# A votes product moved within its step, gate operations reordered on GpSimd and VectorE, and one weight split moved behind a block's rows

## The chip, the cores and the metric

The kernel runs on one core of one Trainium2 chip. The metric is the device time in microseconds of one execution; of several executions the median is given. Engines are called as in the profile: PE (TensorE, matmuls), PEld (its weight loads), DVE (VectorE), ACT (ScalarE), POOL (GpSimd), SP (SyncE, which issues the DMAs).

## The reference, cut to what matters

Attention over pooled keys is followed by a mixture of experts in which each token goes to one expert.

```python
# attention: B=4, N=12288 queries, C=128; kv 384 x 32 positions, pooled 4 x 4 to 768 keys
kv_flat = kv_pool.reshape(B, -1, C) @ w_sr          # keys and values alike
s = scale * (q @ k.transpose(0, 2, 1))
a = np.exp(s - s.max(-1, keepdims=True)); a /= a.sum(-1, keepdims=True) + 1e-09
x = a @ v                                            # rows of 128, 49152 of them
# experts: E=8, F=1024
logits = x @ w_gate                                  # 8 logits a row
expert_idx = np.argmax(logits, axis=1)
gate_w = softmax(logits)[row, expert_idx]
y = gate_w * (np.maximum(x @ w1[expert], 0) @ w2[expert])
```

## The kernel before, in words

**Blocks and slices.** The 49152 rows are 96 blocks of 512 rows, 24 for each batch; a block is four slices of 128 rows. For a slice, PE multiplies the queries by the 768 keys into a score tile `s` of two PSUM halves (columns 0 to 383 of each half; there are two such tiles, used in turn). The columns from 384 on are free, and small products of other work are put there: `beside(t, c, part, ...)` registers a part that is called while slice c of block t issues its scores, and hands it those columns as a place. Then DVE takes the row maximum `nmax` (L361), ACT the exponential `a` (L368), the cast to float16 `ah` is done by ACT in even slices (L391) and by POOL in odd ones (L389), POOL makes the remainder (L393), and a transposing DMA on SP's queue (L394) brings both to `aT`. Two steps later the values' product follows (`block_values`: `m<-aT,v_sb`), and then the logits of the block.

**Steps.** After a start of eight short steps, a step t of nominal length `LEN` = 18.7 computes the scores of block t, the values of block t-2 and the experts of block t-8 (`LAG` = 8). The experts' work of a block is eight hidden products (`hidden_sum`, `hidden_high` = hh on ACT, `hidden_low` = hl on DVE), each followed by a second product (`moe_second`, into `y`). Hidden products, values and logits share three PSUM banks named `m`. The finished block is turned by a DMA (`planes`, `yT`), joined to rows by POOL (`block_join`, L594 twice), scaled by POOL (L598) and written by a DMA of SP (`block_out`).

**Groups.** Four blocks are a group (two at a few places). All rows of a group are first tried with one expert, the one with most votes; rows that chose another are done at the end in a tail. A group's gate runs in parts, one for each call of `gate_part`. In `gate_apart`, which all groups from the third on use: POOL adds to the sums (L466); DVE takes the maxima of the logits (L468); POOL subtracts, compares and multiplies (L470 to L472); DVE takes the index (L474) and the one-hot table (L475); a reciprocal (L477); a POOL product (L479); an exponential; and a few more. `group_count` sums the table (L715, `count`), `group_votes` is the small PE product that adds the counts over the partitions, into the columns beside a slice's scores; `group_first` reads it with five small DVE operations (L724 to L729) and leaves `first_i`, which `group_load` reads on SP to issue the loads of the expert's w1 and w2 (L510, L511). `weight_scales` and `split_expert` then make the float16 halves w1h, w1l, w2h, w2l (`split_part`; the low halves by POOL, L528, in two instructions each). The first two groups use the older `gate`, in which all these operations but the exponential are on DVE (L434 to L454).

**The order** of all instructions is written out by hand. `at(time, part, ...)` puts a part into a heap by a nominal time, and `run` calls the parts in the order of those times (equal times in the order of registration). So the time fixes the place of an instruction in the queues of its engines, each of which runs in order; it is no wait and no real time. In `plan_group`, T is the start of a step, t the step in which a group's last values come; the votes fall into step t+1. The first group has `plan_first`; the second has the branch `t < LAG`, whose T is the ninth step; 22 groups take the general branch; the last one is handled in the tail loop behind the last step. Parts of the main loop that the change's times stand among, with their nominal times in the step: last cast of the step before -0.4 and its remainder +0.45; hidden sums 1.05, 2.35, 4.7, 7.95, 10.3; slices' scores 0, 3.65, 9.25, 14.85 and their maxima 1.08 later; hl 2.4, 3.7, 6.05, 9.3; `q_scale_scores` (L325) 5.95; values 6.0 and 11.6; `planes` 6.02; `q_max` 7.35; `q_turn` 8.0; rows 15.3, 16.0 and 16.85.

## Time and profile before

| | |
|---|---|
| median of 3 runs | 1863.18 us (1863.13 to 1863.6) |
| the profiled execution | 1862.85 us, its span 1861.1 us |
| granted clock of PE | 0.998 |
| busy: PE, POOL, DVE, ACT | 1820.6, 1392.6, 1438.9, 1375.9 us |

The profile is one execution. A row of the order of time has the start and the length in us, the engine, the line, the operation, out<-in, the shapes, and in brackets how long the engine had been idle and what ended that; a row of the waits has who waited for whom, the total in us, the times and the longest. Gaps under 0.15 us are not counted as waits. The ends of matmuls are modelled and overlap the next ones.

### The profile page before, as it was taken

To read this page: it belongs to the slowest core of one execution; us is meant where nothing else is said; L and a number is where in the kernel's file an instruction comes from. 1 tells how busy PE (TensorE), PEld (TensorE's weight loads), DVE (VectorE), ACT (ScalarE), POOL (GpSimd) and SP (SyncE) were. 2 spreads that over 40 slices of the span, in tenths; PEclk is the share of its full clock that TensorE was granted. 3 is DMA by queue.
4 is the path that set the end of the run, shared out by engine and by line. 5 is a ranking of instruction groups with operands and counts; after the bars stand their busy time and mean duration, and the time that the engine had idled before them with its cause. 6 is when DMAs were issued, how large, how long until landed. Compare 5 with 4: busy or idle time off the path is not lost. (4 is left out here: it accounts for less than half of the span.)

```text
span 1861.1 us, 30957 instructions
## 1 busy us (share of the span) xinstructions
PE 1820.6 (98%) x9959; PEld 925.2 (50%) x9959; DVE 1438.9 (77%) x3016; ACT 1375.9 (74%) x2432; POOL 1392.6 (75%) x1521
## 2 busy tenths in 40 slices
PE   6999999999999999999999999999999999999998
PEld 6654444444454544444444444544444444444444
DVE  6887877887788787777787878877777677787586
ACT  3777867777877878877777777787777786877665
POOL 2769788778878878778688797787786877777643
PEclk9999999999999999999999999999999999999999
DMA  6988889777988987778878887777787777776552
GB/s 185 175 157 161 185 162 180 156 128 161 192 176 155 184 161 131 154 149 151 166 152 186 161 171 150 140 152 153 131 157 149 131 145 150 138 148 138 97 144 55
DMA packets 994837, 284.74 MB, mean 153 GB/s; under 512 B 900432, under 2 KB 979922, under 8 KB 994672
## 3 DMA queue, kind: packets, MB, share of 16 engines
q1 hardware_dynamic: 994544, 282.65, 77.7%
q8 instruction: 79, 1.29, 0.3%
q14 instruction: 86, 0.70, 0.1%
q0 software_dynamic: 128, 0.10, 0.0%
HBM read 80.42 MB, written 28.45 MB: 59 GB/s over the span
## 5 line engine op out<-in xcount | busy, mean ns | idle before, releaser
L393 POOL TENSOR_TENSOR ah<-a,ah 128x768 f16<-128x768 f32 x379 | 622.2, 1649 | 184.5 <-ACT ah L391 137.6
L549 ACT ACTIVATE hh<-m 128x512 f16<-128x512 f32 x776 | 459.5, 593 | 353.7 <-PE m L147 349.3
L555 DVE SCALAR_TENSOR_TENSOR hl<-m,hh 128x512 f16<-128x512 f32 x776 | 526.9, 680 | 166.3 <-ACT hh L549 160.0
L147 PE MATMUL s<-k_sb,qh 128*128 128x384 f16 (+1 forms) x2316 | 448.1, 329 | 10.0 <-ACT a L368 6.9
L361 DVE TENSOR_REDUCE nmax<-s 128x1 f32<-128x768 f32 x386 | 367.8, 953 | 41.9 <-PE s L147 28.7
L368 ACT ACTIVATE a<-s,nmax,qs 128x768 f32<-128x768 f32 x348 | 346.7, 996 | 49.7 <-DVE qs L152 21.2
L147 PE MATMUL m<-aT,v_sb 128*128 128x512 f16 x1584 | 370.6, 379 | 0.0
L147 PE MATMUL m<-xh,w1h 128*128 128x512 f16 x776 | 292.1, 376 | 3.4 <-DVE hl L555 3.4
L147 PEld LDWEIGHTS <-qh 128*128 128x128 f16 x2100 | 205.3, 98 | 175.6 <-DVE qs L152 3.9
L147 PE MATMUL m<-xh,w1l 128*128 128x512 f16 x776 | 292.5, 377 | 0.0
L147 PE MATMUL m<-xl,w1h 128*128 128x512 f16 x776 | 292.4, 377 | 0.0
L147 PE MATMUL y<-hh,w2h 128*128 128x512 f16 x768 | 290.8, 379 | 0.7 <-ACT y L588 0.7
L147 PE MATMUL y<-hl,w2h 128*128 128x512 f16 x768 | 291.1, 379 | 0.3 <-DVE hl L555 0.3
L147 PE MATMUL y<-hh,w2l 128*128 128x512 f16 x768 | 291.1, 379 | 0.0
L147 PEld LDWEIGHTS <-v_sb 128*128 128x128 f16 x1764 | 169.9, 98 | 201.9 <-issue 1.8
L147 PEld LDWEIGHTS <-w2h 128*128 128x128 f16 x1536 | 149.5, 98 | 180.4 <-issue 1.0
L147 PEld LDWEIGHTS <-w1h 128*128 128x128 f16 x1552 | 135.4, 97 | 120.7 <-issue 12.2
L389 POOL CAST ah<-a 128x768 f16<-128x768 f32 x185 | 152.7, 826 | 48.6 <-ACT a L368 46.4
L391 ACT CAST ah<-a 128x768 f16<-128x768 f32 x194 | 161.8, 834 | 2.0
L594 POOL COPY o<-yT 128x512 uint16<-128x512 uint16 x190 | 136.3, 764 | 33.8 <-DMA yT<-y 33.7
L409 DVE SCALAR_TENSOR_TENSOR xl<-m,xs,xh 128x512 f16<-128x512 f32 x88 | 66.1, 751 | 116.8 <-ACT xh L404 115.3
L653 POOL TENSOR_TENSOR qh<-qT,qh 128x512 f16<-128x512 f32 (+1 forms) x95 | 111.2, 1170 | 31.2 <-ACT qh L648 31.1
(252 smaller groups left out, 2044.5 us busy)
## 6 DMA issues: line engine op xcount, KB each, us to landing
kv_raw<-in_moe_w_dram SPq DMA_DIRECT2D x54, 512.0 KB, 4.8
out_dram<-o SPq DMA_DIRECT2D x96, 256.0 KB, 2.4
q_sb<-in_q_dram SPq DMA_DIRECT2D x380, 64.0 KB, 2.5
kv_raw<-in_kv_dram SPq DMA_DIRECT2D x72, 256.0 KB, 4.4
aT<-ah SPq DMA_TRANSPOSE x379, 3.8
aT<-in_kv_dram SPq DMA_DIRECT2D x8, 512.0 KB, 9.3
kv_raw<-in_kv_dram SPq DMA_DIRECT2D x4, 512.0 KB, 5.6
k_dram<-k_sb SPq DMA_DIRECT2D x8, 192.0 KB, 2.7
```

Of the source, the lines that this page charges most:

```text
L147: return nc.tensor.matmul(o, l, r, start=start, stop=stop)
L361: nc.vector.tensor_reduce(nmax, pss[:, :, :KH], axis=AX.XY, op=ALU.max, negate=True)
L368: nc.scalar.activation(a.rearrange("p (h k) -> p h k", h=2), pss[:, :, :KH], AF.Exp, bias=nmax, scale=units[c] if units else 1.0, accum_ou ...
L389: nc.gpsimd.tensor_copy(ah[:, 0], a)
L391: nc.scalar.copy(ah[:, 0], a)
L393: nc.gpsimd.tensor_sub(ah[:, 1], a, ah[:, 0])
L409: nc.vector.scalar_tensor_tensor(xl[:, :n], po[:, :n], k["xs"][:, 0:1], xh[:, :n], op0=ALU.mult, op1=ALU.subtract)
L549: nc.scalar.activation(hh[:, :n], ph[:, :n], AF.Relu)
L555: nc.vector.scalar_tensor_tensor(hl[:, :n], ph[:, :n], 0.0, hh[:, :n], op0=ALU.max, op1=ALU.subtract)
L594: nc.gpsimd.tensor_copy(o.bitcast(U16).rearrange("p c (d i) -> p i c d", i=2)[:, i], yT.rearrange("p (i c) d -> p i c d", i=2)[:, i])
L653: by.tensor_sub(ql, BL[t].pop("qT"), qh)
```

## The change

Four edits, all of them to nominal times, so to places in the order; two more lines split one registration into two.

```diff
@@ plan_group, t < LAG: second group, ninth step
             at(begin(LAG - 1) + 4.64, gate_part, g)
-            for _ in range(5):
-                at(T + 3.5, gate_part, g)
-            at(T + 6.1, group_count, g)
+            for time in (3.75, 3.75, 3.75, 5.0, 5.0):
+                at(T + time, gate_part, g)
+            at(T + 5.0, group_count, g)
             beside(LAG, 2, group_votes, g)
@@ plan_group, all other groups (22)
         T += LEN
-        at(T + 0.3, gate_part, g)
+        at(T - 0.42, gate_part, g)
         at(T + 2.45, gate_part, g)
         at(T + 2.5, group_count, g)
-        beside(t + 1, 1, group_votes, g)
-        at(T + 5.8, group_first, g)
-        at(T + 5.85, gate_part, g)
+        beside(t + 1, 1, lambda pv: G[g].update(place=pv))
+        at(T + 5.95, lambda: group_votes(g, G[g].pop("place")))
+        at(T + 6.9, group_first, g)
+        at(T + 6.95, gate_part, g)
         at(T + 7.1, group_load, g)
@@ plan_weights; late is the second group alone, T is the tenth step
         at(T + 14.95, split_part, g, 0)
-        at(T + (15.25 if late else 16.8), split_part, g, 0)
+        at(T + (16.9 if late else 16.8), split_part, g, 0)
```

- In the ninth step, hl of the second hidden product (3.7) now stands ahead of the second group's gate on DVE (maxima, difference, compare at 3.75); index, table and count come at 5.0, behind slice 1's maximum (4.73) and q's scale (4.9).
- In the 22 groups, POOL's L470 to L472 stand ahead of the cast of the last slice of the step before (-0.4), not between that cast and its remainder.
- In the same groups, the votes product keeps its place in slice 1's score tile but is issued at 5.95, behind the third hidden product and the second product after it, directly ahead of the values (6.0). `group_first` and the reciprocal L477 move behind `q_scale_scores` and the third hl.
- In the tenth step, POOL's two instructions for w1l of the second group stand behind the join and the scaling of the first block's rows.

## The prediction

> **What bounds the kernel now.** I read the page first, then the chain of PE's waits, then the order of time around one votes product. PE is the bound:

> ```profile
> PE 1820.6 (98%) x9959; PEld 925.2 (50%) x9959; DVE 1438.9 (77%) x3016; ACT 1375.9 (74%) x2432; POOL 1392.6 (75%) x1521
> ...
> PE s L147 <- DVE count L715: 5.1, 6, 1.3
> ```

> Between the ninth step and the tail loop PE stands still almost only in front of the votes product, the matmul that reads `count`. So 5.1 us (with two shorter waits 5.4) is all that its move can bring. A PE delay inside a step is a delay of the end: no later PE gap takes it up.

> **The votes product in an ordinary group** (columns: start, length, engine, line):

> ```profile
> 1558.04 0.29 DVE L468 TENSOR_REDUCE gate<-lg 128x16 f32<-128x128 f32 x1
> 1558.13 0.82 POOL L389 CAST ah<-a 128x768 f16<-128x768 f32 x1 [0.58 <-ACT a L368]
> 1558.92 0.41 POOL L470 TENSOR_TENSOR gate_d<-lg,gate 128x128 f32<-128x128 f32 x1
> 1560.04 0.45 POOL L472 TENSOR_TENSOR gate_d<-gate_d,iota_e 128x128 f32<-128x128 f32 x1
> 1560.45 1.65 POOL L393 TENSOR_TENSOR ah<-a,ah 128x768 f16<-128x768 f32 x1
> 1561.58 0.67 DVE L475 TENSOR_TENSOR gate_d<-gate,iota_e 128x128 f32<-128x128 f32 x1
> 1562.75 0.17 PE L147 MATMUL s<-count,ones_q 128*128 128x8 bf16 x1
> 1563.17 0.95 DVE L361 TENSOR_REDUCE nmax<-s 128x1 f32<-128x768 f32 x1
> 1564.07 2.10 PE L147 MATMUL m<-aT,v_sb 128*128 128x512 f16 x9
> 1564.94 0.15 DVE L728 TENSOR_SCALAR first_i<-votes 128x1 int32<-128x1 f32 x1
> 1565.37 1.40 SPq L590 DMA_TRANSPOSE yT<-y  x1
> 1567.94 0.39 SPq L510 DMA_DIRECT2D kv_raw<-in_moe_w_dram  x1
> ```

> Here the product waits for nothing. The change puts it straight in front of the values' product (1564.07) and, in the program's order, behind slice 1's row maximum L361, which ends at 1564.12. Both touch the same score tile: L361 reads columns 0 to 383 of each half, the product writes columns from 384 on. Does the product then wait for L361? No row of before has a PE write behind a DVE read of other columns of a tile. The nearest ones:

> ```profile
> ACT a L368 <- DVE qs L152: 22.6, 26, 1.4
> ACT a L368 <- DVE votes L729: 1.4, 1, 1.4
> ...
> DVE nmax L361 <- PE s L202: 6.6, 13, 0.6
> ```

> The exponential L368 reads scores alone, yet waits for L152 and L729, DVE reads of the spare columns of its tile; L361 waits for a product written there (L202). So order is kept by the tile, even read after read, and I take it that the product waits for L361.

> [...]

> **GpSimd's gate operations ahead of the cast.** POOL was idle 0.58 before the cast, but the gate operations need L468's maxima, which end at 1558.33. POOL after DVE costs about 0.05 (an estimate from DVE to PE in the ninth step below), so they run from 1558.38 for 1.57 (1558.92 to 1560.49), to 1559.95. The cast, begun 0.04 before that end as such neighbours are here, ends at 1560.73; the subtraction L393, which now follows its own input, starts 0.08 later (the gap from L594 to L598 in the last fence) and ends at 1562.46 instead of 1562.10. L475, with two SBUF inputs, ends 0.15 after L393 both here (1562.25) and in the next fences: it is held while L393 runs. So L475, and behind it the count, hl and L361 without a pause, come 0.35 later: L361 ends at 1564.47, the product starts at 1564.52 and the values at 1564.55, **+0.48**. Twelve groups are of this kind, +0.46 to +0.49 each: +5.9. In three more a values' subtraction stands ahead of L361:

> ```profile
> 1195.29 0.95 DVE L361 TENSOR_REDUCE nmax<-s 128x1 f32<-128x768 f32 x1
> ...
> 1195.98 1.24 PE L147 MATMUL m<-aT,v_sb 128*128 128x512 f16 x5
> ```

> 1196.24 + 0.35 + 0.08 is 0.69 behind 1195.98: +2.1 for three. Without POOL's 0.35 the ordinary group still pays 0.13 and these 0.34, the lower bound.

> **Groups in which PE waited** (seven, in steps that also fold or project keys):

> ```profile
> 1041.54 0.82 POOL L389 CAST ah<-a 128x768 f16<-128x768 f32 x1
> 1042.89 0.69 DVE L555 SCALAR_TENSOR_TENSOR hl<-m,hh 128x512 f16<-128x512 f32 x1
> 1043.86 1.65 POOL L393 TENSOR_TENSOR ah<-a,ah 128x768 f16<-128x768 f32 x1
> 1044.25 1.40 DVE L475 TENSOR_TENSOR gate_d<-gate,iota_e 128x128 f32<-128x128 f32 x1
> 1046.12 0.17 PE L147 MATMUL s<-count,ones_q 128*128 128x8 bf16 x1 [0.97 <-DVE count L715]
> 1046.58 0.95 DVE L361 TENSOR_REDUCE nmax<-s 128x1 f32<-128x768 f32 x1
> 1047.43 2.10 PE L147 MATMUL m<-aT,v_sb 128*128 128x512 f16 x9
> ```

> POOL has no idle time here, so the swap leaves L393's end but for the 0.12 between cast and subtraction. The 0.97 goes, and the wait for L361 takes its place: 1047.53 + 0.12 + 0.08 = 1047.73, 0.30 later than 1047.43. Six groups give +0.30 to +0.48 by the same sum, +2.2. This one is special: the gate operations end 0.8 earlier, so L474 and L475 follow hl at about 1043.85, while the cast runs (to 1043.91), and L475 can slip in ahead of L393. Then L361 is early, nothing waits, and the group gains 0.97. I count the slip (the ninth step shows one); without it, +0.30.

> Sum of the 22 groups: 5.9 + 2.1 + 2.2 - 1.0 = **+9.2** (3.8 without POOL's delay, as the lower end; 10.5 without the slip).

> What follows costs nothing: `group_first` moves behind hl, so `first_i` comes about 1.1 later (1565.09 to about 1566.2), still before SP is through with the yT transposes (1566.77) that stand ahead of its load of the expert; PE has 2.1 of values to run meanwhile. The capture of the place issues nothing. If that cover went, the load at 1567.94 would shift by the same time.

> **Ninth step.**

> ```profile
> 112.32 2.37 POOL L528 TENSOR_TENSOR w2l<-kv_raw,w2h 128x512 f16<-128x512 f32 x2
> 112.55 1.13 DVE L441 SCALAR_TENSOR_TENSOR gate_d<-gate_d,iota_e 128x128 f32<-128x128 f32 x1
> 114.75 0.68 DVE L555 SCALAR_TENSOR_TENSOR hl<-m,hh 128x512 f16<-128x512 f32 x1
> 115.49 0.38 PE L147 MATMUL m<-xh,w1h 128*128 128x512 f16 x1 [1.39 <-DVE hl L555]
> 116.97 0.72 ACT L640 ACTIVATE q_sb<-q_sb,qs 128x512 f32<-128x512 f32 x1 [3.99 <-DVE qs L321]
> 117.60 0.58 ACT L549 ACTIVATE hh<-m 128x512 f16<-128x512 f32 x1
> 118.21 0.69 DVE L555 SCALAR_TENSOR_TENSOR hl<-m,hh 128x512 f16<-128x512 f32 x1 [1.02 <-ACT hh L549]
> 118.82 0.37 DVE L715 TENSOR_REDUCE count<-gate_d 128x8 bf16<-128x128 f32 x1
> 119.24 0.17 PE L147 MATMUL s<-count,ones_q 128*128 128x8 bf16 x1 [1.26 <-DVE count L715]
> ```

> L441 ended at 113.68, just behind the first of L528's two halves: the slip. Now hl (114.75) goes ahead of the gate and PE's 1.39 disappears. But DVE still does three gate operations before the row maximum and q's scale, so ACT's L640 and hh come only about 0.5 earlier. `count` (from about 117.25) no longer waits for hl, but the next hidden product needs the bank that this hl frees, at about 118.5 instead of 118.9. Of 2.65 us of waits, 0.3 to 0.9 is gained; I take **-0.7**.

> **Second group's w1 behind the rows.**

> ```profile
> 146.63 2.27 POOL L528 TENSOR_TENSOR w1l<-kv_raw,w1h 128x512 f16<-128x512 f32 x2
> 148.85 1.43 POOL L594 COPY o<-yT 128x512 uint16<-128x512 uint16 x2
> 150.36 1.04 POOL L598 TENSOR_TENSOR o<-o,cover 128x512 f32<-128x512 f32 x1
> ...
> 147.84 0.10 PEld L147 LDWEIGHTS <-w1l 128*128 128x128 f16 x1 [0.28 <-POOL w1l L528]
> ...
> 166.27 0.99 PE L147 MATMUL s<-k_sb,qh 128*128 128x384 f16 x5 [1.09 <-POOL qh L653]
> ```

> The first weights of w1l are loaded the moment its first half is done. With 1.43 + 0.08 + 1.04 of row work ahead, that half ends near 150.3: PE stands 2.5. Later 1.1 of this comes back: at 166.27 PE waited 1.09 for POOL's queue, whose work up to there is the same. **+1.4** (2.5 if nothing comes back; 0.7 for both parts together when POOL's queue moves up with the ninth step's gain, which I take).

> **Sum**: 9.2 - 0.7 + 1.4 = +9.9 us on the profiled 1862.85 (span 1861.1), so 1872.8; the median of the runs, 1863.18, stands 0.33 above, so 1873.1.

> **Rivals.** *POOL hides the swap*: the gate operations delay L393 nowhere. For it: idle 0.58; against: L468's end. Groups +3.8, total +4.5: 1867.7. *The product doesn't wait for L361*, its order being kept by columns: then the seven waits vanish and POOL's 0.35 is covered, since even the latest count is ready about when PE gets there; -4.1 + 0.7 = -3.4: 1859.8, not slower. It decides at the start of the moved product: before L361's end or behind it. Against it: the three rows on the score tile. *The w1 order costs nothing*, if the tail of POOL's queue has moved ahead of PE: 9.2 - 0.7 = +8.5, 1871.7, still slower. *More comes behind*: the slip fails and the ninth step gains nothing: 10.5 + 2.5 = +13: 1876.

> **How the numbers follow.** A measurement tells about 0.2% (3.7 us) from no change. Forecast with its w1 variant 0.68, hidden swap 0.12, more behind 0.06, product without wait 0.10 (on the edge of 0.2%, so halved), mixtures near zero 0.04. Slower 0.86, same 0.09, faster 0.05. The range takes in the hidden swap less 1 us for its latencies and the worst sum plus 1: 1866.5 to 1877.

> **What would show it.** Right: PE waiting on `DVE nmax L361` in front of the votes product about 21 times, 0.4 to 1.5 each; waits on count gone but in the ninth step; L393 in front of L475 ending 0.3 later; in the eleventh step a w1l load that waits about 2 us. Wrong: a votes product that starts while L361 runs.

## The result, and the profile after

Slower by 0.6%. Four runs of the changed kernel had a median of 1875.8 us (1874.09 to 1877.36) beside 1863.39 us (1863.13 to 1865.64) for the kernel before: a ratio of 1.0063, 95% interval 1.0051 to 1.0075. The forecast was 1873.1 in a range of 1866.5 to 1877. The profiled execution took 1876.2 us, its span 1874.4 instead of 1861.1: +13.3 us, where the sum had +9.9.

The page and PE's waits of the changed kernel (total us, times, longest):

```profile
PE 1828.4 (98%) x9959; PEld 927.6 (49%) x9959; DVE 1446.5 (77%) x3016; ACT 1376.8 (73%) x2432; POOL 1393.3 (74%) x1521
...
PE s L147 <- DVE nmax L361: 10.9, 22, 1.4
...
PE m L147 <- DVE hl L555: 2.9, 5, 0.9
PE m L147 <- POOL w1l L528: 2.3, 1, 2.3
...
PE s L147 <- DVE count L715: 0.8, 1, 0.8
```

Before, PE waited 5.1 us in six places for `count`. One such wait is left, in the ninth step. In its place stands a wait for slice 1's row maximum, L361, in all 22 groups that take the general branch, 10.9 us in sum. The third new line is PE's wait for w1l.

The same ordinary group as in the prediction; PE comes to it 11.57 us later than before:

```profile
1569.61 0.29 DVE L468 TENSOR_REDUCE gate<-lg 128x16 f32<-128x128 f32 x1
1569.98 0.41 POOL L470 TENSOR_TENSOR gate_d<-lg,gate 128x128 f32<-128x128 f32 x1 [0.86 <-DVE gate L468]
...
1571.51 0.82 POOL L389 CAST ah<-a 128x768 f16<-128x768 f32 x1
...
1572.41 1.64 POOL L393 TENSOR_TENSOR ah<-a,ah 128x768 f16<-128x768 f32 x1
...
1573.16 1.04 DVE L475 TENSOR_TENSOR gate_d<-gate,iota_e 128x128 f32<-128x128 f32 x1
...
1575.13 0.94 DVE L361 TENSOR_REDUCE nmax<-s 128x1 f32<-128x768 f32 x1
...
1576.13 0.17 PE L147 MATMUL s<-count,ones_q 128*128 128x8 bf16 x1 [0.35 <-DVE nmax L361]
1576.20 1.64 PEld L147 LDWEIGHTS <-v_sb 128*128 128x128 f16 x9 [0.70 <-issue]
1576.23 2.10 PE L147 MATMUL m<-aT,v_sb 128*128 128x512 f16 x9
```

POOL, which had its cast to do first before, now stands idle 0.86 us for the maxima (L468). L393 ends at 1574.05, which is 0.38 later than before when the 11.57 are taken off; L475 is held to 1574.20; L361 ends at 1576.07. The product starts 0.06 behind it, the values 0.10 behind the product. Without the 11.57 the values stand at 1564.66 instead of 1564.07: 0.59 lost here, by starts of other matmuls 0.58.

PE's delay against before, read off as the difference in the start of the same matmul on both sides of each place:

| place | forecast, us | measured, us |
|---|---|---|
| start-up, to 73 us | 0 | +0.64 |
| ninth step | -0.7 | -0.94 |
| second group's w1 | +1.4 | +2.80 |
| 12 ordinary groups | +5.9 | +7.0 (0.58 each) |
| 3 groups with a values' subtraction | +2.1 | +2.3 |
| 6 groups in which PE had waited | +2.2 | +2.0 |
| the group at 1046.12 | -1.0 | -0.55 |
| sum | +9.9 | +13.3 |

The first row is not the change's: up to 73 us the two kernels issue the same instructions. All eight experiments also came 0.24 to 1.20 us later than the profile of before at that place, e7_ninth_bank least and e4_w1 most. The granted clock differs there from execution to execution; how much of the delay it makes isn't shown, since e2_gate and e3_ninth had one slow stretch of 3.41 us there, as before had, and still came 0.71 and 0.46 later. Stretches from 37 to 44 us, of before and then of the changed kernel (the clock is the third number from the end):

```profile
37.00:44.00 7.00, 5.46 (x28) 5.20 (x27) 5.69 (x11) 4.67 (x9) 3.45 (x4) 0.76 1.11 176
```

```profile
37.00:44.00 7.00, 6.22 (x24) 5.76 (x25) 5.69 (x10) 4.64 (x9) 3.56 (x3) 0.52 1.08 177
```

So a difference of a microsecond between two profiled executions of these kernels means nothing until the first 73 us are taken off, and that is done below.

### The profile page after: what moved, and what is told of

It is laid out like the page before. It is cut to its first block, busy times and chain, and to the rows that moved or that the text cites. A ratio compares the mean times of both kernels' runs of the same rounds, so it can differ in the third digit from the quotient of the medians.

```text
span 1874.4 us, 30957 instructions
## 1 busy us (share of the span) xinstructions
PE 1828.4 (98%) x9959; PEld 927.6 (49%) x9959; DVE 1446.5 (77%) x3016; ACT 1376.8 (73%) x2432; POOL 1393.3 (74%) x1521
## 5 line engine op out<-in xcount | busy, mean ns | idle before, releaser
L393 POOL TENSOR_TENSOR ah<-a,ah 128x768 f16<-128x768 f32 x379 | 622.2, 1649 | 178.2 <-ACT ah L391 133.4
L549 ACT ACTIVATE hh<-m 128x512 f16<-128x512 f32 x776 | 459.7, 594 | 371.5 <-PE m L147 366.7
L555 DVE SCALAR_TENSOR_TENSOR hl<-m,hh 128x512 f16<-128x512 f32 x776 | 527.3, 681 | 174.8 <-ACT hh L549 168.2
L147 PE MATMUL s<-k_sb,qh 128*128 128x384 f16 (+1 forms) x2316 | 449.1, 330 | 8.5 <-ACT a L368 6.5
L361 DVE TENSOR_REDUCE nmax<-s 128x1 f32<-128x768 f32 x386 | 367.9, 953 | 43.1 <-PE s L147 29.4
L368 ACT ACTIVATE a<-s,nmax,qs 128x768 f32<-128x768 f32 x348 | 346.8, 996 | 47.4 <-DVE qs L152 21.5
L147 PE MATMUL m<-aT,v_sb 128*128 128x512 f16 x1584 | 370.5, 379 | 0.0
L147 PE MATMUL m<-xh,w1h 128*128 128x512 f16 x776 | 292.5, 377 | 2.9 <-DVE hl L555 2.9
L147 PE MATMUL m<-xh,w1l 128*128 128x512 f16 x776 | 293.0, 378 | 2.3 <-POOL w1l L528 2.3
L147 PE MATMUL m<-xl,w1h 128*128 128x512 f16 x776 | 292.7, 377 | 0.0
L147 PE MATMUL y<-hh,w2h 128*128 128x512 f16 x768 | 291.2, 379 | 0.7 <-ACT y L588 0.7
L147 PEld LDWEIGHTS <-qh 128*128 128x128 f16 x2100 | 205.3, 98 | 174.3 <-DVE qs L152 3.7
L147 PE MATMUL y<-hl,w2h 128*128 128x512 f16 x768 | 291.3, 379 | 0.3 <-DVE hl L555 0.3
L147 PE MATMUL y<-hh,w2l 128*128 128x512 f16 x768 | 291.3, 379 | 0.0
L147 PEld LDWEIGHTS <-v_sb 128*128 128x128 f16 x1764 | 168.3, 98 | 215.3 <-issue 19.2
L147 PEld LDWEIGHTS <-w2h 128*128 128x128 f16 x1536 | 149.8, 98 | 180.8 <-issue 1.8
L147 PEld LDWEIGHTS <-w1h 128*128 128x128 f16 x1552 | 137.1, 98 | 116.0 <-issue 5.8
L389 POOL CAST ah<-a 128x768 f16<-128x768 f32 x185 | 152.6, 825 | 41.9 <-ACT a L368 40.1
L594 POOL COPY o<-yT 128x512 uint16<-128x512 uint16 x190 | 136.1, 763 | 32.3 <-DMA yT<-y 32.3
L653 POOL TENSOR_TENSOR qh<-qT,qh 128x512 f16<-128x512 f32 (+1 forms) x95 | 111.2, 1170 | 31.8 <-ACT qh L648 30.1
```

Of the source, the lines that this page charges most:

```text
L147: return nc.tensor.matmul(o, l, r, start=start, stop=stop)
L361: nc.vector.tensor_reduce(nmax, pss[:, :, :KH], axis=AX.XY, op=ALU.max, negate=True)
L368: nc.scalar.activation(a.rearrange("p (h k) -> p h k", h=2), pss[:, :, :KH], AF.Exp, bias=nmax, scale=units[c] if units else 1.0, accum_ou ...
L389: nc.gpsimd.tensor_copy(ah[:, 0], a)
L393: nc.gpsimd.tensor_sub(ah[:, 1], a, ah[:, 0])
L549: nc.scalar.activation(hh[:, :n], ph[:, :n], AF.Relu)
```

## The experiments

Theory A after this result: the time is lost in the groups, where the votes product now waits for a reader of other columns of its score tile and the swap on POOL makes that reader later, and some 3 us behind w1's wait with its slow stretch. Rival B: the order isn't kept by the tile, so the moved product by itself costs nothing, and the swap on POOL or the w1 order makes the loss. The first four kernels do one part of the change each, on one chip, where the kernel before ran 24 times with a median of 1864.36 us.

**e1_votes**, the votes product alone, POOL's order and the rest as before:

```diff
-        beside(t + 1, 1, group_votes, g)
-        at(T + 5.8, group_first, g)
-        at(T + 5.85, gate_part, g)
+        beside(t + 1, 1, lambda pv: G[g].update(place=pv))
+        at(T + 5.95, lambda: group_votes(g, G[g].pop("place")))
+        at(T + 6.9, group_first, g)
+        at(T + 6.95, gate_part, g)
```

> Only the votes product, group_first and L477 move. Theory A (the product waits for slice 1's row maximum L361, since both touch one score tile): no shift of POOL, so an ordinary group loses about 0.2 us (1564.12 + 0.06 + 0.10 against 1564.07), the three with a values' subtraction 0.4, the seven that waited 0.25 each: +5.5 us, about 1869, and PE's wait names L361. Rival B (order by columns; PE waited in the changed kernel because POOL had made the counts late): with POOL as before nothing waits and the 5.4 us of waits go, -4 us, about 1859.

Measured: 1870.48 us (1868.7 to 1871.44), ratio 1.0035 (1.0021 to 1.005). PE's waits:

```profile
PE s L147 <- DVE nmax L361: 4.8, 7, 1.3
```

The ordinary groups lose 0.21 each, the three 0.38 to 0.39, those that had waited between 0.02 and 0.76 (expected were 0.25 each); the 58th step's group (1046.12 before) gains 0.93; +4.6 in sum. The waits in the ordinary groups are under 0.15 and so not in this line. The move alone makes the kernel slower, as theory A had it, and the rival by columns falls: by it the waits would be gone.

**e2_gate**, POOL's gate operations ahead of the cast alone:

```diff
-        at(T + 0.3, gate_part, g)
+        at(T - 0.42, gate_part, g)
```

> Only POOL's gate operations go ahead of the cast; the product stays beside slice 1. If the swap delays L393 and with it L475 by 0.35 in an ordinary group, the count comes 0.35 later and the product in its old place waits for it: 0.3 each in 12 groups, 0.1 in three, up to 0.15 in the crowded ones, one of which gains: +4 us, about 1867. If POOL's idle time hides the swap: no change, and L475 ends where it did.

Measured: 1868.67 us (1867.6 to 1871.6), ratio 1.0027 (1.0016 to 1.0038).

```profile
PE s L147 <- DVE count L715: 7.4, 18, 1.3
```

Ordinary groups lose 0.33 each, the three 0.18, those that had waited between -0.14 and +0.62; the 58th step's gains 1.13; +4.5 in sum. The swap delays L475 and so `count`, and the product, still in its old place, now waits for it 18 times instead of six. In an ordinary group the two parts alone cost 0.21 + 0.33 = 0.54, together 0.58: they add, because the swap delays the chain L475, count, hl, L361, and the move puts the product behind the end of that chain.

**e3_ninth**, the ninth step's gate alone:

```diff
-            for _ in range(5):
-                at(T + 3.5, gate_part, g)
-            at(T + 6.1, group_count, g)
+            for time in (3.75, 3.75, 3.75, 5.0, 5.0):
+                at(T + time, gate_part, g)
+            at(T + 5.0, group_count, g)
```

> Only the second group's gate in the ninth step. From the two traces: -0.95 us by the end of that step, kept to the end: 1862.4, less than these runs can tell; read from the trace. Rival: the gain is taken back at the wait for the twelfth step's queries (POOL), then -0.0 behind it.

Measured: 1863.68 us (1861.97 to 1868.09), ratio 1.0 (0.9991 to 1.001): no difference that this measurement can tell. In the trace PE gains 0.96 in the ninth step (from 0.46 late to 0.50 early). Then the groups in which PE waits scatter by up to 0.5 either way, and behind the last group it stands 0.03 early. Measured from the 0.46 at the start, 0.49 of the 0.96 is left, so neither the expectation (all of it kept) nor its rival (none) came true. The rest went where PE waits for DVE.

**e4_w1**, the second group's w1 alone:

```diff
-        at(T + (15.25 if late else 16.8), split_part, g, 0)
+        at(T + (16.9 if late else 16.8), split_part, g, 0)
```

> Only w1l of the second group behind the rows. Theory A: PE waits 2.5 us for w1l, then its matmuls run at half the clock for about 3.3 us (another 1.6), and 1.1 comes back where PE waited for POOL in the twelfth step: +2.9, about 1866.3. Rival: the half clock in the changed kernel's profile had nothing to do with the wait: +1.4, about 1864.8, with the granted clock at 1.0 behind the wait.

Measured: 1865.37 us (1863.82 to 1868.49), ratio 1.001 (1.0 to 1.002). PE's wait is the one of the changed kernel. POOL and PE there, in order of time:

```profile
150.32 2.27 POOL L528 TENSOR_TENSOR w1l<-kv_raw,w1h 128x512 f16<-128x512 f32 x2
...
151.54 0.39 PE L147 MATMUL m<-xh,w1l 128*128 128x512 f16 x1 [2.29 <-POOL w1l L528]
```

The first half is done near 151.5 and PE goes on at once. PE is 2.45 later behind it and gets back 1.25 at the twelfth step's queries, where it no longer waits for POOL's L653: +1.2, close to the +1.4 forecast; at the end PE is 1.1 later than at 73 us. But in the changed kernel the same wait was followed by slow matmuls, and here it wasn't: the half clock that theory A expected didn't come. PE's order in the changed kernel:

```profile
150.07 0.61 PE L147 MATMUL m<-xh,w1l 128*128 128x512 f16 x1 [2.30 <-POOL w1l L528]
150.47 0.63 PE L147 MATMUL y<-hh,w2h 128*128 128x512 f16 x1
```

The matmuls come 0.40 to 0.43 apart and last 0.61 to 0.63, where they come 0.22 apart and take 0.38 behind the wait of e4_w1. That costs 1.6 us by the start of the matmuls behind it.

**e6_w1_cast**: the w1 part moved further, behind the cast too, everything else as before; meant to make the wait longer and so the slow stretch certain. One run.

```diff
-        at(T + (15.25 if late else 16.8), split_part, g, 0)
+        at(T + (18.35 if late else 16.8), split_part, g, 0)
```

> Before, with w1l of the second group one place further back than in the change, behind the cast as well. PE waits 3.3 us for it. Theory A (the granted clock is set window by window, 3.41 us long, from how busy PE was in the window before; the change's 2.3 us of idling fell into one window, the same wait with w1 alone into two): 3.3 us fill most of one window wherever it begins, so half the clock for 3.41 us behind the wait, +1.7. Rival: the slow window of the changed kernel was chance and has nothing to do with idling: clock 1.0 behind the wait.

Measured: 1864.81 us, where the kernel before had a median of 1863.88 in 25 runs on that chip. PE waited 3.05 us, yet the clock stayed at full speed, so this expectation failed as well. What tells the three kernels apart is where the wait falls. In the records of the granted clock the slow stretches begin a multiple of 3.41 us apart within a run (in the changed kernel at 37.23 and at 149.87, 33 such windows later), each run with its own phase. Cut along that grid, two windows of the changed kernel, two of e4_w1 and two of e6_w1_cast (PE's busy time stands behind the length, the clock third from the end):

```profile
146.46:149.87 3.41, 1.32 (x8) 0.50 (x6) 2.67 (x8) 3.38 (x5) 3.33 (x4) 1.00 1.26 188
149.87:153.28 3.41, 3.21 (x8) 1.19 (x9) 0.78 (x2) 1.60 (x5) 3.33 (x4) 0.50 0.83 168
```

```profile
147.26:150.67 3.41, 1.99 (x11) 0.87 (x9) 2.49 (x5) 3.38 (x6) 3.33 (x5) 1.00 1.18 122
150.67:154.08 3.41, 2.54 (x13) 1.23 (x14) 1.37 (x7) 2.80 (x6) 3.33 (x4) 1.00 1.03 225
```

```profile
147.05:150.46 3.41, 2.14 (x12) 0.90 (x10) 2.46 (x6) 3.38 (x7) 3.33 (x5) 1.00 1.10 146
150.46:153.87 3.41, 1.63 (x8) 0.80 (x9) 1.38 (x6) 2.04 (x3) 3.41 (x4) 1.00 1.00 213
```

In the changed kernel 2.1 of the 2.30 us of waiting fell into one window, and the next one ran at half clock. In e4_w1 the 2.29 us fell on two windows (1.42 and 0.87), in e6_w1_cast the 3.05 us too (1.28 and 1.77), and nothing followed. These three cases fit this reading, and e5_bank below is a fourth; no run set the phase on purpose.

**e5_bank**: the whole change, but the votes product goes, at the same place in the order, into one of the banks of the hidden products instead of its score tile. Nothing else in the order differs, so it decides what makes the product wait.

```diff
-        beside(t + 1, 1, lambda pv: G[g].update(place=pv))
-        at(T + 5.95, lambda: group_votes(g, G[g].pop("place")))
+        at(T + 5.95, lambda: group_votes(g, bank(T + 5.95, T + 7.8)))
```

(This diff is against the changed kernel.)

> The whole change, but the votes product goes at the same place in the order (5.95) into one of the three banks m and not beside slice 1's scores. Theory A (the wait for L361 is kept by the score tile): the waits on L361 vanish although L361 ends as late as in the changed kernel; ordinary groups lose 0, the crowded ones gain what they waited, -4 us over the groups; with -0.95 of the ninth step and +1.2 to +2.8 of w1: 1860 to 1862. Rival B (PE waits there for the count, or anything else that is late in front of the values): still 0.35 of wait in each ordinary group, about 1875.

Measured: 1859.38 us (1858.69 to 1862.08), ratio 0.998 (0.9971 to 0.9989). An ordinary group in order of time:

```profile
1558.04 1.05 DVE L475 TENSOR_TENSOR gate_d<-gate,iota_e 128x128 f32<-128x128 f32 x1
1559.12 0.38 DVE L715 TENSOR_REDUCE count<-gate_d 128x8 bf16<-128x128 f32 x1
1560.02 0.95 DVE L361 TENSOR_REDUCE nmax<-s 128x1 f32<-128x768 f32 x1
1560.51 0.17 PE L147 MATMUL m<-count,ones_q 128*128 128x8 bf16 x1
1560.54 2.10 PE L147 MATMUL m<-aT,v_sb 128*128 128x512 f16 x9
```

L475 is as late as in the changed kernel and held as long (1.05), but the product starts in the middle of L361 and PE waits for nothing. Ordinary groups cost 0.00, the ones in which PE had waited gain 0.29 to 1.13 each, in sum -4.6. The tile of the product is what turned the groups from +10.8 in the changed kernel to -4.6; with another tile the same order makes the kernel faster, though the w1 part, which costs 1.2, is still in it. (The median lies 0.6 under the 1860 to 1862 that were expected.)

That w1 costs 1.2 and not 2.8 here is the clock's doing again. PE waits 2.27 us for w1l, and 1.87 of them fall into one window, which lies almost as in the changed kernel. PE was busy for 1.53 us in it, where it had been 1.32, and the clock stayed at full speed:

```profile
146.44:149.85 3.41, 1.53 (x9) 0.65 (x7) 2.70 (x7) 3.38 (x5) 3.33 (x5) 1.00 1.24 167
149.85:153.26 3.41, 3.02 (x16) 1.52 (x17) 1.46 (x4) 2.82 (x6) 3.33 (x4) 1.00 0.93 190
```

But PE's busy time alone doesn't tell the cases apart. In the start-up of e4_w1 a busier window was followed by half clock:

```profile
34.63:38.04 3.41, 1.82 (x9) 1.51 (x10) 3.27 (x8) 2.77 (x5) 3.41 (x3) 1.00 0.39 74
38.04:41.45 3.41, 2.42 (x11) 2.06 (x10) 2.94 (x5) 1.70 (x4) 2.25 (x2) 0.50 1.25 178
```

**e7_ninth_bank** and **e8_ninth_early** keep what was good. Both take the ninth step's edit, leave POOL's order and w1 as before, and move the product: e7 as in e5, e8 within its score tile, but ahead of slice 1's L361 in the order, with `group_first` left at its old time. The move of e8 against before:

```diff
-        beside(t + 1, 1, group_votes, g)
+        beside(t + 1, 1, lambda pv: G[g].update(place=pv))
+        at(T + 4.72, lambda: group_votes(g, G[g].pop("place")))
```

> Before with the ninth step's edit and the votes product at 5.95 in a bank m (group_first at 6.9); POOL's order and w1 as before. Theory A: the groups' waits on the count vanish (-4.1) and nothing takes their place, ninth step -0.95: about 5 us below before. Rival: a bank taken out of the three in rotation makes the hidden products wait for hl instead: no gain.

> Before with the ninth step's edit and the votes product in its score tile at 4.72, behind the third hidden product but ahead of slice 1's row maximum in the order; group_first as before (5.8). Theory A: now L361 waits for the product and not the product for L361: PE's waits on the count shrink by 0.65 each (5.1 to about 1.3), L361 starts 0.2 to 0.3 later in ordinary groups at no cost: -3 -0.95, about 4 us below before. Rival: DVE's delay comes back to PE through hl and the banks: no gain.

Measured: e7 1859.25 us (1858.29 to 1860.56), ratio 0.9977 (0.9968 to 0.9986); e8 1858.72 us (1858.07 to 1861.37), ratio 0.9974 (0.9964 to 0.9984). An ordinary group of e8:

```profile
1558.25 0.39 DVE L715 TENSOR_REDUCE count<-gate_d 128x8 bf16<-128x128 f32 x1
1559.38 0.17 PE L147 MATMUL s<-count,ones_q 128*128 128x8 bf16 x1
1559.61 0.96 DVE L361 TENSOR_REDUCE nmax<-s 128x1 f32<-128x768 f32 x1 [0.38 <-PE s L147]
1560.05 2.10 PE L147 MATMUL m<-aT,v_sb 128*128 128x512 f16 x9
```

Here the order is turned round: L361 waits 0.38 for the product, and PE waits for nothing. The groups in which PE had waited gain 0.28 to 0.91, -4.2 in sum (-3.6 in e7), the ordinary ones 0.00. This is the fastest version that was run, by 0.26% against before and by 17 us against the changed kernel, though those two did not run side by side. Between e7 and e8 the intervals don't decide.

## Why the prediction was right, and where it was not

**The wait for L361: right.** It was put 21 times at 0.4 to 1.5 us; there were 22 from 0.3 to 1.4 us. The step that carried the forecast, that a tile's order holds for columns that L361 doesn't read, is shown by e5_bank against the changed kernel: same place in the order, another tile, and no wait where there had been 0.35 us in an ordinary group. The other tile lies in another PSUM bank as well, so no run here tells an order kept by the tile from one kept by the bank.

**The ordinary group: mis-sized, 0.48 for 0.58.** Three small terms were short: L475's end moved by 0.38, not 0.35 (POOL started 0.08 behind L468, 1569.90 to 1569.98, where 0.05 had been taken); the product starts 0.06 behind L361, not 0.05; and the values start 0.10 behind the product, not 0.03. The last makes most of it: the first weights of the values are loaded 0.07 behind the product's start (the row of v_sb at 1576.20). In e5_bank, where nothing waits, the two matmuls are 0.03 apart (1560.51 and 1560.54). The wait alone doesn't make this tenth. In e2_gate the product, in its old place, waits as well, and the next matmul, with other weights, starts 0.02 behind it:

```profile
1567.63 0.17 PE L147 MATMUL s<-count,ones_q 128*128 128x8 bf16 x1 [0.17 <-DVE count L715]
...
1567.65 0.38 PE L147 MATMUL m<-xh,w1h 128*128 128x512 f16 x1
```

Why the weights of v_sb come later there stays open. The same tenth made e1_votes cost 0.21 in an ordinary group where the prediction had 0.13 without POOL's part.

**POOL hides nothing of the swap: right**, in its place and its size. e2_gate, the swap alone, costs 0.33 in an ordinary group.

**The 58th step's group: the gain came, for another reason.** Forecast -0.97 by L475 slipping in ahead of L393. The changed kernel, where PE is 8.40 later than before:

```profile
1051.30 0.69 DVE L555 SCALAR_TENSOR_TENSOR hl<-m,hh 128x512 f16<-128x512 f32 x1
1051.46 1.65 POOL L393 TENSOR_TENSOR ah<-a,ah 128x768 f16<-128x768 f32 x1
...
1052.22 1.04 DVE L475 TENSOR_TENSOR gate_d<-gate,iota_e 128x128 f32<-128x128 f32 x1
...
1055.19 0.17 PE L147 MATMUL s<-count,ones_q 128*128 128x8 bf16 x1 [0.35 <-DVE nmax L361]
```

L475 began inside L393 and was held to its end, so the slip, the step that the prediction counted on, failed here. But L393 itself ends at 1044.71 without the 8.40, 0.80 earlier than before (1045.51). The kernel before had this on POOL ahead of the cast:

```profile
1038.78 1.43 POOL L594 COPY o<-yT 128x512 uint16<-128x512 uint16 x2 [1.24 <-DMA yT<-y]
```

In the changed kernel POOL comes to that copy with no idle time (1045.66), its rows being there; why they are there earlier isn't shown. e1_votes has POOL as early at this place, again with no idle time, and gains 0.93 without the swap. The wait on L361 is left, 0.35, and the gain is 0.55.

The slip itself exists. In e2_gate, where POOL is as late at this place as before (it stands idle 1.10 ahead of L594), L475 of this group begins ahead of L393, takes 0.29 and is not held; the group gains 1.13:

```profile
1047.62 0.29 DVE L475 TENSOR_TENSOR gate_d<-gate,iota_e 128x128 f32<-128x128 f32 x1
1047.79 1.64 POOL L393 TENSOR_TENSOR ah<-a,ah 128x768 f16<-128x768 f32 x1
```

In e5_bank it slips too (0.43, begun 0.37 ahead of L393). So the prediction had the mechanism right and POOL's place against DVE wrong.

**The first of the six groups that had waited** (189.98 before) gained 0.25 instead of losing 0.4: PE came to it already 2.5 us late behind w1, so DVE and POOL were less behind. e4_w1 bears this out: there w1 alone takes 0.84 off this group, whose wait is gone. The other five lost 0.36 to 0.52, near the 0.30 to 0.48 forecast.

**The ninth step: -0.94 for -0.7.** hl's wait of 1.39 went as forecast and that on count shrank from 1.26 to 0.83. A new wait of 0.87 for hl stands behind it, which is the bank that the step named:

```profile
112.95 0.69 DVE L555 SCALAR_TENSOR_TENSOR hl<-m,hh 128x512 f16<-128x512 f32 x1 [0.88 <-ACT hh L549]
114.31 1.13 DVE L441 SCALAR_TENSOR_TENSOR gate_d<-gate_d,iota_e 128x128 f32<-128x128 f32 x1
...
117.93 0.17 PE L147 MATMUL s<-count,ones_q 128*128 128x8 bf16 x1 [0.83 <-DVE count L715]
118.96 0.38 PE L147 MATMUL m<-xh,w1h 128*128 128x512 f16 x1 [0.87 <-DVE hl L555]
```

Of the 2.65 us that PE waited here, 1.70 are left.

**w1: the step that failed most, +2.8 for +1.4.** The wait made PE 2.45 later (2.5 forecast) and 1.25 came back (1.1 forecast). What the step lacked is the half clock behind the wait, +1.6. e4_w1, with the same wait and a full clock, costs 1.2. Of the four traces with such a wait, one paid the 1.6, and in that one 2.1 us of the wait fell into one window; in the other three at most 1.87 did. How often a run of the changed kernel pays it, its one trace can't tell.

**The load of the expert comes no later: right.**

```profile
1579.46 0.39 SPq L510 DMA_DIRECT2D kv_raw<-in_moe_w_dram  x1
```

Less 11.57 this is 1567.89, where before it was 1567.94. The cover named, SP's yT transposes ahead of it, holds.

So the +3.4 by which the sum fell short are 1.4 of w1, 1.6 of the groups and 0.6 of the start-up, less 0.2 of the ninth step.

## What to carry to other kernels

Before a small product is moved into the spare columns of a tile, list who else reads or writes that tile and where its new place falls among them: behind a DVE read PE waited here for the read to end (22 times, 0.3 to 1.4 us), ahead of it DVE waited (0.38 us in e8_ninth_early), which cost nothing, and in another bank nobody waited (e5_bank). The whole change made this kernel 0.6% slower; the same order with the product in another bank made it 0.2% faster; and with the product ahead of the read, POOL's order and w1 as before, it was 0.26% faster. And price a PE wait of a few us by more than its length: a wait of 2.3 us cost 1.2 us in e4_w1, with the clock at 1.00 behind it, and 2.8 in the changed kernel, with a window at 0.50 behind it.

## What the runs showed of the hardware

**L475, once begun inside L393, is held for as long as L393 runs.** It takes 0.67 us when it starts late in L393, 1.04 us in the changed kernel's ordinary groups and 1.40 us in the 58th step before. In all 22 groups of both kernels it ends 0.08 to 0.15 us behind L393. So where L393 ended 0.38 later, in the changed kernel's ordinary group, L475 did too; that is how e2_gate's 0.37 on POOL reaches PE. Begun 0.17 us ahead of L393, as in the 58th step of e2_gate, it took 0.29 us and wasn't held.
